# The exponential's bias taken from the maximum's own instruction, and the reciprocals' spread moved from POOL's queue to SP's

## The chip, the cores and the metric

The kernel runs on one core of one Trainium2 chip. Its time is the device time of one execution in microseconds (us); of the kernel before there are three runs, with a median of 543.97 us (543.92 to 544.14), and one execution that was also traced.

The engines are called PE (matrix multiplications), DVE (vector engine), ACT (scalar engine, here the exponential and the copies out of PSUM), POOL (a second, slower elementwise engine that also issues DMAs) and SP (which here only issues DMAs). Each runs its own list of instructions strictly in order, and waits at an instruction until the semaphores that it names have arrived.

## The reference

Three layers in a row, on 2 sequences of 768 tokens: attention with 8 heads of 64, then two mixing layers of width 512.

```
q_bits = q @ proj > 0 ; k_bits = k @ proj > 0       # 6 bits each
scores = where(q_bits == k_bits, q @ k.T / 8, -1e9) # per head, 768 x 768
attn   = exp(scores - max(scores)) ; attn /= sum(attn) + 1e-9
x      = attn @ v                                   # heads put side by side
x      = sigmoid(xr @ w_r) * (relu(xk @ w_k)**2 @ w_v)     # xk, xr mix x with the token before
h      = relu(x @ w_in) ; u, v = halves(h)
out    = (u * (w_spatial @ norm(v) + b)) @ w_out
```

The mask needs no step of its own in the kernel: signs of the projected bits stand as 12 more rows beside the 64 rows of keys and queries, scaled so that a pair of rows whose bits differ comes out of the matrix multiplication lower by 2**31 for each bit.

## The kernel before, in words

`attention` treats two heads at a time (a pair; there are 8 pairs). The work is cut into 96 units: 128 queries of one head against all 768 keys. For unit i, four functions follow each other on different engines:

- `scores(i)`: four matrix multiplications on PE into a PSUM tile `s` (two such tiles exist; lines 374 to 385).
- `peak(i)`, line 392: one DVE instruction copies `s` into an SBUF tile `p` and gives the row maximum `m` with it. `bias(i)`, line 400: a second DVE instruction, on one number per row, makes `nb`, which is `m` times -1/8.
- `expo(i)`, line 410: one ACT instruction turns `p` into exp(p/8 + nb) in place, and adds up each row into `den`.
- `transp` and `evac`, lines 420 and 426: PE transposes `p` in two halves of three blocks, and ACT copies each half from PSUM into `PT`. `av3`, line 455, then multiplies by the values, 12 matrix multiplications for half a group of 6 units.

After an opening that is written out (the string `head`), a loop runs over p = 3 to 31, three units per step. Its order is the same in each step: scores of two units, then peaks, exponentials and transposes one unit behind, `av3`, the third unit. A table `plan` adds jobs to a step: for the weights of the later layers (`weight_jobs`, lines 36 to 81: a load by SP, then ACT line 41, DVE lines 44, 49, 55, 62 and 65, ACT line 71 and two subtractions on POOL, lines 76 and 77), and for the next pair (loads by POOL, lines 239, 251 and 252, sign bits, and eight subtractions `split_piece` on POOL, line 263).

For every second step the sums of a group are inverted: `recip` (lines 435, 436, 438 on DVE, then four small DMAs by SP to DRAM, line 441), one step later `spread` (line 448: two DMAs that read that DRAM back, broadcast over 64 partitions each, into `rb`), and again a step later `finish` (line 467 on DVE: output times `rb`). Where p % 4 is 1 SP issues the spread, and where p % 4 is 3 POOL does, ahead of the jobs of the step. POOL's issue waits until the four small DMAs have landed.

`mixers` holds the two later layers; none of its code is touched.

Of the kernel before, what the change touches and what calls it, by code (L numbers as in the profile page):

```python
# [10 lines left out]
F32 = mybir.dt.float32  # L11
F32R = mybir.dt.float32r
AF = mybir.ActivationFunctionType
ALU = mybir.AluOpType
AX = mybir.AxisListType

B, H, S, D = 2, 8, 768, 64
NP = H // 2
HS = S // 2
# [3 lines left out]
BIG = float(2 ** 30)  # L23
# [59 lines left out]
def hash_attention_moe_kernel(  # L83
# [134 lines left out]
    with tc.manual_schedule():  # L218
        attention(**env)
        mixers(**env)  # L220


def attention(tc, nc, mid, dram, ident, msc, omu, misc, cst_sb, pb, epsT, kq, vP, XT, TK0, wr, w_r, wk,
              w_k, w_v, ps_s, ps_t, obank, mix_jobs, r_group, tick, now, at_tick, plan_weight, wv, **_):
    PS = bass.MemoryType.PSUM
    with ExitStack() as ctx:
        at = ctx.enter_context(tc.tile_pool(name="at", bufs=1))
# [142 lines left out]
        P, PT, den, S_ps, C_sb, R = {}, {}, {}, {}, {}, {}  # L370

        def scores(i):
            g, u = divmod(i, 6)
            pp, half = divmod(g, 2)
            e, j = divmod(u, 3)
            t = TK[pp % 2][e]
            q0 = half * HS + 128 * j
            s = ps_s.tile([128, 2, 512], F32, tag="s", name="s")
            for n in range(2):
                w = t[:, 3 - n, q0:q0 + 128]  # L380
                for c in range(2):
                    nc.tensor.matmul(  # L382
                        s[:, c, :HS], w, t[:, n, c * HS:(c + 1) * HS],
                        start=(n == 0), stop=(n == 1),
                    )
            S_ps[i] = s

        def peak(i):
            s = S_ps.pop(i)
            c = at.tile([128, 2, HS], F32, tag="p", bufs=3, name="p")  # L390
            m = at.tile([128, 1], F32, tag="m", bufs=4, name="m")
            nc.vector.tensor_scalar(  # L392
                c, s[:, :, :HS], -BIG / 2, None, op0=ALU.max, op1=ALU.max, accum_out=m
            )
            C_sb[i] = (c, m)

        def bias(i):
            c, m = C_sb[i]
            nb = at.tile([128, 1], F32, tag="nb", bufs=4, name="nb")
            nc.vector.tensor_scalar(nb, m, -0.125, None, op0=ALU.mult)  # L400
            C_sb[i] = (c, nb)

        def expo(i):
            g, u = divmod(i, 6)
            c, nb = C_sb.pop(i)
            if u == 0:
                den[g] = at.tile([128, 6], F32, tag="den", bufs=2, name="den")
                PT[g] = mid.tile([128, 2, 6, HS], F32, tag="PT", bufs=2, name="PT")
            c = c.rearrange("p c n -> p (c n)")
            nc.scalar.activation(  # L410
                c, c, AF.Exp, bias=nb, scale=0.125, accum_out=den[g][:, u:u + 1]
            )
            P[i] = c

# [18 lines left out]
        def recip(g):  # L433
            rc = rcs[g % 2]
            nc.vector.tensor_scalar_add(rc[:, 0:6], den.pop(g), 1e-9)
            nc.vector.reciprocal(rc[:, 0:6], rc[:, 0:6])
            rt = at.tile([128, 32], F32, tag="rt", bufs=2, name="rt")
            nc.vector.transpose(rt, rc)  # L438
            ds = dram.tile([6, 128], F32, tag="ds", name="ds")
            for n in range(4):  # L440
                nc.sync.dma_start(ds[:, 32 * n:32 * n + 32], rt[32 * n:32 * n + 6, :])
            R[g] = ds

        def spread(g, eng):
            ds = R[g]
            R[g] = at.tile([128, 3, 128], F32, tag="rb", bufs=2, name="rb")
            for e in range(2):
                eng.dma_start(
                    R[g][64 * e:64 * e + 64],
                    ds[3 * e:3 * e + 3].unsqueeze(0).to_broadcast([64, 3, 128]),  # L450
                )
# [11 lines left out]
        def finish(g):  # L463
            pp, half = divmod(g, 2)
            b, p = divmod(pp, NP)
            PT.pop(g)
            nc.vector.tensor_mul(
                XT[:, p, b, 1 + half * HS:1 + (half + 1) * HS],
                obank[:, :HS],
                R.pop(g).rearrange("p n q -> p (n q)"),  # L470
            )
# [15 lines left out]
        def plan_wv():  # L487
            for h in range(2):
                wv.append(mid.tile([128, 2, 4, DM], F32R, tag="PT", bufs=2, name="wv"))
                for c in range(4):  # L490
                    n = 4 * h + c
                    if not n:
                        at_tick(1, early[4])
                        at_tick(2, early[7])
                        continue
                    plan_weight(
                        (0, 0, 2, 8, 16, 18, 20, 22)[n], (wv[h][:, 0, c, :], wv[h][:, 1, c, :]),
                        w_v[128 * n:128 * n + 128],
                    )
# [13 lines left out]
        for n in range(12):  # L513
            dst, src, c, o = units[n]
# [49 lines left out]
        def av3(p):  # L564
            for n in range(3):
                av(p // 2, 3 * (p % 2) + n)

        def move(i, c, copy=nc.scalar.copy):
            evac(i, c, transp(i, c), copy)

        def score(i):
            peak(i)
            bias(i)

        ts = {}

        def group(k):
# [2 lines left out]
        def from_group(k, copy=nc.scalar.copy):  # L580
            evac(k // 2, k % 2, ts.pop(k), copy)

        def slot(n):
            for job in plan.pop((n // 10, n % 10), ()):
                job()

        step = {
            "S": scores, "K": score, "X": expo, "T": group, "E": from_group,
            "V": lambda k: from_group(k, nc.vector.tensor_copy), "J": slot, "Z": bits_mm, "G": bits_signs,
            "L": lambda e: split_part(0, e, 0, nc.vector), "R": recip, "P": lambda e: bits_place(1, (e,)),  # L590
        }
# [9 lines left out]
        for p in range(3, np3):  # L601
            a = 3 * p
            scores(a)
            scores(a + 1)
            score(a)
            if p > 3:
                move(a - 2, 1)
                expo(a)
                move(a - 1, 0)
                move(a - 1, 1)  # L610
            else:
                move(a - 1, 0)
                expo(a)
                move(a - 1, 1)
            score(a + 1)
            for job in plan.pop((p, 2), ()):
                job()
            expo(a + 1)
            av3(p - 3)
            if p % 2 == 0:  # L620
                recip(p // 2 - 1)
            if p % 4 == 3:
                spread((p - 3) // 2, nc.gpsimd)
            for job in plan.pop((p, 0), ()):
                job()
            if p % 4 == 1:
                spread((p - 3) // 2, nc.sync)
            if p >= np3 - 2:
                tick()
            scores(a + 2)  # L630
            move(a, 0)
            move(a, 1)
            score(a + 2)
            expo(a + 2)
            if p >= 4 and p % 2 == 0:
                finish((p - 4) // 2)
            move(a + 1, 0)
            for job in plan.pop((p, 1), ()):
                job()
            if p == np3 - 2:  # L640
                plan_wv()
            if p >= np3 - 2:
                tick()
# [323 lines left out]
```

## Time and profile before

| | kernel before |
|---|---|
| median of 3 runs | 543.97 us |
| the traced execution | 544.15 us |
| span of its instructions | 542.4 us |
| PE busy | 535.8 us, 99% |
| DVE busy | 379.1 us, 70% |
| ACT busy | 339.9 us, 63% |
| POOL busy | 151.9 us, 28% |
| granted clock of PE | full speed in all 40 slices of the span |

Busy shares are averages over the span. DVE and ACT are at 80 to 100% in the first 40% of it, which is the attention, and far lower behind it. A matrix multiplication is recorded with a modelled end, so rows of PE overlap a little; the start of one row against the start of the next says more than a row's length. "Idle before" in brackets names what ended an engine's wait, by the semaphore that came last.

### The profile page before, as it was taken

How to read it: one execution, taken by the hardware profiler on the slowest of the kernel's cores; microseconds unless marked ns; L12 is line 12 of the kernel's file. 1: busy time of each engine (PE TensorE's matmuls, PEld its weight loads, DVE VectorE, ACT ScalarE, POOL GpSimd, SP SyncE). 2: the span in 40 equal slices, each digit the busy share in tenths (PEclk: the TensorE clock that was granted, in tenths of full speed). 3: DMA queues.
4: the chain of work that ended last, by engine and by line, in shares of the span. 5: the costliest groups of instructions: out<-in, count | busy, mean ns of one | idle time of the engine just before them, and what ended most of it. 6: DMA issues, size and time to landing. Idle time of an engine off the chain costs nothing.

```text
span 542.4 us, 8997 instructions
## 1 busy us (share of the span) xinstructions
PE 535.8 (99%) x3174; PEld 462.4 (85%) x3174; DVE 379.1 (70%) x815; ACT 339.9 (63%) x722; POOL 151.9 (28%) x171
## 2 busy tenths in 40 slices
PE   8999999999999999999999999999999999999997
PEld 6777676767676767699999999999998999899896
DVE  8888979898979899477787776127996784443240
ACT  8988888888888889588645839147345342321211
POOL 7939585959595923100000000000200000000000
PEclk9999999999999999999999999999999999999999
DMA  8694939493949402111131111001662100001102
GB/s 245 125 231 95 242 82 228 94 246 79 233 92 250 107 24 93 55 40 39 40 116 36 44 39 40 0 1 40 211 216 78 44 25 1 2 19 40 58 21 97
DMA packets 19596, 51.10 MB, mean 94 GB/s; under 512 B 3776, under 2 KB 5984, under 8 KB 19552
## 3 DMA queue, kind: packets, MB, share of 16 engines
q0 software_dynamic: 6816, 20.45, 18.0%
q1 hardware_dynamic: 12304, 29.80, 17.6%
q8 instruction: 25, 0.41, 0.3%
q10 hardware_dynamic: 432, 0.28, 0.2%
q14 instruction: 19, 0.16, 0.1%
HBM read 46.29 MB, written 3.19 MB: 91 GB/s over the span
## 4 chain that ended last, share of the span: by engine, by line
PE 91%; DVE 5%; POOL 1%; issue 1%; ACT 1%; DVEq 0%; ACTq 0%
PE o L176 12%; PE o L455 11%; PE s L382 11%; PE k L176 11%; PE t L420 10%; PE v L721 9%; PE s L176 7%; PE w L176 6%; PE r L176 5%; PE u L176 5%; PE o L721 3%; DVE p L392 2%; PE z L280 1%; POOL tk L323 1%; ACT p L410 1%
## 5 line engine op out<-in xcount | busy, mean ns | idle before, releaser
L392 DVE TENSOR_SCALAR_CACHE_REDUCE p<-s 128x768 f32<-128x768 f32 x96 | 91.7, 955 | 19.5 <-PE s L382 17.0
L410 ACT ACTIVATE p<-p,nb 128x768 f32<-128x768 f32 x96 | 90.6, 943 | 9.6 <-DVE nb L400 8.4
L426 ACT COPY PT<-t 128x384 f32<-128x384 f32 x189 | 82.7, 476 | 16.0 <-PE t L420 15.0
L382 PE MATMUL s<-tk 128*128 128x384 f32 x384 | 85.9, 355 | 1.1 <-DVE p L392 0.7
L382 PEld LDWEIGHTS s<-tk 128*128 128x128 f32 x384 | 63.5, 188 | 21.3 <-DVE rt L438 6.0
L420 PE MATMUL t<-ident,p 128*128 128x128 f32 x576 | 76.5, 275 | 1.0 <-ACT p L410 0.7
L420 PEld LDWEIGHTS t<-ident,p 128*128 128x128 f32 x576 | 66.1, 141 | 7.8 <-ACT p L410 4.0
L455 PE MATMUL o<-PT,v 128*64 128x384 f32 x384 | 68.8, 494 | 0.0
L176 PE MATMUL k<-tk,wk 128*128 128x384 f32 x336 | 59.6, 334 | 0.0
L263 POOL TENSOR_TENSOR tk<-x,tk 64x384 fp32r<-64x384 f32 x56 | 58.4, 1073 | 1.0
L176 PEld LDWEIGHTS k<-tk,wk 128*128 128x128 f32 x336 | 58.4, 188 | 0.0
L721 PE MATMUL v<-k,wv 128*128 128x384 f32 x288 | 53.6, 334 | 0.0
L721 PEld LDWEIGHTS v<-k,wv 128*128 128x128 f32 x288 | 50.3, 188 | 0.0
L780 POOL DMA_DIRECT2D wsp<-in_w_spT_dram x6 | 3.6, 618 | 165.8 <-DVE w_a L44 159.3
L455 PEld LDWEIGHTS o<-PT,v 128*64 128x64 f32 x384 | 24.8, 136 | 28.6 <-issue 28.2
L176 PE MATMUL o<-wk,tk 128*128 128x512 f32 (+1 forms) x168 | 36.2, 374 | 0.0
L176 PEld LDWEIGHTS o<-wk,tk 128*128 128x128 f32 x168 | 30.0, 188 | 5.5
L702 ACT ACTIVATE kr<-k 128x384 f32<-128x384 f32 x28 | 13.6, 487 | 29.6 <-PE k L176 29.4
L121 ACT CAST tk<-g 128x384 fp32r<-128x384 f32 x16 | 8.2, 514 | 37.5 <-DVE g L851 37.5
L176 PE MATMUL w<-wk,tk 128*128 128x512 f32 x132 | 30.7, 390 | 0.0
L176 PE MATMUL r<-tk,wr 128*128 128x384 f32 x168 | 30.6, 337 | 0.0
L687 DVE TENSOR_TENSOR k<-kt,k 128x384 fp32r<-128x384 f32 x32 | 17.8, 555 | 17.9 <-ACT k L705 17.6
(117 smaller groups left out, 878.9 us busy)
## 6 DMA issues: line engine op xcount, KB each, us to landing
tk<-in_kq_dram POOLq DMA_DIRECT2D x30, 384.0 KB, 9.0
x<-in_kq_dram POOLq DMA_DIRECT2D x6, 768.0 KB, 7.8
w_raw<-in_w_k_dram SPq DMA_DIRECT2D x8, 512.0 KB
w_raw<-in_w_v_dram SPq DMA_DIRECT2D x8, 512.0 KB
w_raw<-in_w_in_dram SPq DMA_DIRECT2D x8, 512.0 KB
v<-in_vP_dram SPq DMA_DIRECT2D x8, 384.0 KB
out_dram<-ot SPq DMA_DIRECT2D x11, 256.0 KB
wsp<-in_w_spT_dram POOLq DMA_DIRECT2D x6, 384.0 KB, 5.1
```

The source lines that it names most:

```text
L121: nc.scalar.copy(hi, src)
L176: nc.tensor.matmul(o, a, x, start=(i == 0), stop=(i == len(seq) - 1))
L263: nc.gpsimd.tensor_sub(tk[l, 1 + 2 * t, o], raw[pp][l, t, o], tk[l, 2 * t, o])
L382: nc.tensor.matmul(s[:, c, :HS], w, t[:, n, c * HS:(c + 1) * HS], start=(n == 0), stop=(n == 1),)
L392: nc.vector.tensor_scalar(c, s[:, :, :HS], -BIG / 2, None, op0=ALU.max, op1=ALU.max, accum_out=m)
L410: nc.scalar.activation(c, c, AF.Exp, bias=nb, scale=0.125, accum_out=den[g][:, u:u + 1])
L420: nc.tensor.transpose(t[:, 128 * n:128 * n + 128], p[:, k0:k0 + 128], ident)
L426: copy(PT[g][:, e, 3 * c:3 * c + 3, 128 * j:128 * j + 128], t[:, :HS].rearrange("p (n q) -> p n q", n=3),)
L455: nc.tensor.matmul(obank[64 * e:64 * e + 64, :HS], vt[g // 2][:, kt, e, :], PT[g][:, e, kt, :], start=(kt == 0), stop=(kt == 5),)
L687: later(lag, lambda: eng.tensor_sub(lo, src, hi))
L702: nc.scalar.activation(r, o[:, :HS], AF.Relu)
L721: nc.tensor.matmul(os[m][:, :HS], w, x, start=(c == 0 and k == 0), stop=(c == 7 and k == 2),)
```

## The change

The first DVE instruction now multiplies the scores by -1/8 and takes the minimum with 2**26 (a bound that only the masked scores reach), and its running result over the row is the minimum: this is already minus the maximum over 8, the bias. `bias` and its tile `nb` are gone, and the exponential runs with scale -1 and bias `m`. Of the spreads that POOL issued, only the one of step 3 stays there; those of steps 7, 11, 15, 19, 23, 27 and 31 are issued by SP, behind the step's jobs.

```diff
             nc.vector.tensor_scalar(
-                c, s[:, :, :HS], -BIG / 2, None, op0=ALU.max, op1=ALU.max, accum_out=m
+                c, s[:, :, :HS], -0.125, BIG / 16, op0=ALU.mult, op1=ALU.min, accum_out=m
             )
-        def bias(i):
-            c, m = C_sb[i]
-            nb = at.tile([128, 1], F32, tag="nb", bufs=4, name="nb")
-            nc.vector.tensor_scalar(nb, m, -0.125, None, op0=ALU.mult)
-            C_sb[i] = (c, nb)
...
             nc.scalar.activation(
-                c, c, AF.Exp, bias=nb, scale=0.125, accum_out=den[g][:, u:u + 1]
+                c, c, AF.Exp, bias=m, scale=-1.0, accum_out=den[g][:, u:u + 1]
             )
...
-            score(a)
+            peak(a)
...
-            if p % 4 == 3:
+            if p == 3:
                 spread((p - 3) // 2, nc.gpsimd)
             for job in plan.pop((p, 0), ()):
                 job()
-            if p % 4 == 1:
+            if p % 2 and p > 3:
                 spread((p - 3) // 2, nc.sync)
```

On DVE, this is the list before from step 7 to the first peak of step 9 (line 392 is the peak, 400 the bias, 62, 65, 44, 49 and 55 the weights, 435 to 438 the inversion):

```order
L62 TENSOR_SCALAR w_p<-w_b 128x512
L392 TENSOR_SCALAR p,m<-s 128x768
L400 TENSOR_SCALAR nb<-m 128x1
L65 SCALAR_TENSOR_TENSOR w_a<-w_raw,w_p 128x512
L392 TENSOR_SCALAR p,m<-s 128x768
L400 TENSOR_SCALAR nb<-m 128x1
L392 TENSOR_SCALAR p,m<-s 128x768
L400 TENSOR_SCALAR nb<-m 128x1
L435 TENSOR_SCALAR rc_90<-den 128x6
L436 RECIPROCAL rc_90<-rc_90 128x6
L438 STREAM_TRANSPOSE rt<-rc_90 128x32
L44 TENSOR_SCALAR w_a<-w_a 128x512
```

And the same place now, where the lines from 400 on have moved up (435 is now 429, 467 now 461):

```order
L62 TENSOR_SCALAR w_p<-w_b 128x512
L392 TENSOR_SCALAR p,m<-s 128x768
L65 SCALAR_TENSOR_TENSOR w_a<-w_raw,w_p 128x512
L392 TENSOR_SCALAR p,m<-s 128x768 x2
L429 TENSOR_SCALAR rc_90<-den 128x6
L430 RECIPROCAL rc_90<-rc_90 128x6
L432 STREAM_TRANSPOSE rt<-rc_90 128x32
L44 TENSOR_SCALAR w_a<-w_a 128x512
```

The biases are gone and nothing else has changed its place on DVE. On POOL, at step 7, the two spread DMAs between the subtractions for the next pair (263) and the load of the pair after it (239) are gone, and the weights' subtractions (76, 77) stand nearer to line 263:

```order
 L263 TENSOR_TENSOR tk_0_77<-x,tk_0_77 64x384 x4
 L263 TENSOR_TENSOR tk_1_78<-x,tk_1_78 64x384 x4
-L448 DMA rb<-ds 64x384 x2
 L239 DMA x<-in_kq_dram 128x2x768
 L76 TENSOR_TENSOR w_b<-w_b,wr 128x512
```

On SP, at the same step, they come in ahead of a weight's load (37) and the values' load (257):

```order
-L441 DMA ds<-rt 6x32 x4
+L435 DMA ds<-rt 6x32 x4
+L442 DMA rb<-ds 64x384 x2
 L37 DMA w_raw<-in_w_r_dram 128x1024
 L257 DMA v<-in_vP_dram 128x768
```

There the two DMAs stand directly behind the four whose data they read (435, 441 before).

## Rows read from the trace of the kernel before

**Rows 1.** The page's chain of waits: shares of the span by engine.

```profile
PE 91%; DVE 5%; POOL 1%; issue 1%; ACT 1%; DVEq 0%; ACTq 0%
```

**Rows 2.** Groups by line: xcount | busy us, mean ns | idle before.

```profile
L392 DVE TENSOR_SCALAR_CACHE_REDUCE p<-s 128x768 f32<-128x768 f32 x96 | 91.7, 955 | 19.5 <-PE s L382 17.0 <-ACT wr L71 1.5
...
L400 DVE TENSOR_SCALAR nb<-m 128x1 f32<-128x1 f32 x96 | 14.8, 154 | 3.3
...
L44 DVE TENSOR_SCALAR w_a<-w_a 128x512 f32<-128x512 f32 x32 | 14.1, 440 | 4.9 <-ACT w_a L41 4.9
```

**Rows 3.** Timeline of PE, line 455: start us, us, engine line operation.

```profile
77.28 2.16 PE L455 MATMUL o<-PT,v 128*64 128x384 f32 x12
...
83.64 2.16 PE L455 MATMUL o<-PT,v 128*64 128x384 f32 x12
...
90.81 2.16 PE L455 MATMUL o<-PT,v 128*64 128x384 f32 x12
...
190.89 2.16 PE L455 MATMUL o<-PT,v 128*64 128x384 f32 x12
...
198.55 2.16 PE L455 MATMUL o<-PT,v 128*64 128x384 f32 x12
...
205.37 2.16 PE L455 MATMUL o<-PT,v 128*64 128x384 f32 x12
```

**Rows 4.** Timeline of one unit's peak, bias and exponential, DVE and ACT.

```profile
62.16 0.95 DVE L392 TENSOR_SCALAR_CACHE_REDUCE p<-s 128x768 f32<-128x768 f32 x1
...
63.03 0.08 DVE L392 DVE_READ_ACCUMULATOR p<-s 128x1 f32 x1
63.15 0.15 DVE L400 TENSOR_SCALAR nb<-m 128x1 f32<-128x1 f32 x1
63.25 0.96 DVE L392 TENSOR_SCALAR_CACHE_REDUCE p<-s 128x768 f32<-128x768 f32 x1
63.52 0.94 ACT L410 ACTIVATE p<-p,nb 128x768 f32<-128x768 f32 x1
```

**Rows 5.** Timeline of DVE and PE from 80 to 89 us, steps 11 and 12.

```profile
80.47 0.96 DVE L392 TENSOR_SCALAR_CACHE_REDUCE p<-s 128x768 f32<-128x768 f32 x1 [1.48 <-ACT wr L71]
...
81.54 0.68 DVE L65 SCALAR_TENSOR_TENSOR w_a<-w_raw,w_p 128x512 f32<-128x512 uint32 x1
...
84.33 0.56 DVE L435 TENSOR_SCALAR rc<-den 128x6 f32<-128x6 f32 x1
...
85.29 1.21 DVE L44 TENSOR_SCALAR w_a<-w_a 128x512 f32<-128x512 f32 x1
...
88.65 0.97 PE L382 MATMUL s<-tk 128*128 128x384 f32 x4 [0.27 <-DVE p L392]
...
88.71 0.56 DVE L467 TENSOR_TENSOR XT<-o,rb 128x384 f32<-128x384 f32 x1
```

**Rows 6.** Timeline of POOL in the same stretch.

```profile
81.64 1.16 POOL L448 DMA_DIRECT2D rb<-ds  x2 [1.79 <-DMA ds<-rt]
...
82.77 0.77 POOL L239 DMA_DIRECT2D x<-in_kq_dram  x1
...
83.54 1.32 POOL L76 TENSOR_TENSOR w_b<-w_b,wr 128x512 f32<-128x512 f32 x1
...
84.93 1.28 POOL L77 TENSOR_TENSOR wr<-w_b,w_a 128x512 fp32r<-128x512 f32 x1
```

**Rows 7.** Timeline of DVE and of POOL at steps 27 and 28.

```profile
188.78 2.22 DVE L65 SCALAR_TENSOR_TENSOR w_a<-w_raw,w_p 128x512 f32<-128x512 uint32 x1
...
193.09 0.16 DVE L435 TENSOR_SCALAR rc<-den 128x6 f32<-128x6 f32 x1
...
189.12 1.32 POOL L76 TENSOR_TENSOR w_b<-w_b,wk 128x512 f32<-128x512 f32 x1
```

**Rows 8.** The chain of waits in the opening: start us, us, what.

```profile
17.51 0.17 DVE nb L400
```

**Rows 9.** Timeline of SP's queue, the spread of step 9.

```profile
67.90 1.27 SPq L448 DMA_DIRECT2D rb<-ds  x2
```

More of the change, by code (lines that the diff above doesn't have):

```diff
@@ L392, in peak @@
             nc.vector.tensor_scalar(
-                c, s[:, :, :HS], -BIG / 2, None, op0=ALU.max, op1=ALU.max, accum_out=m
+                c, s[:, :, :HS], -0.125, BIG / 16, op0=ALU.mult, op1=ALU.min, accum_out=m
             )
             C_sb[i] = (c, m)
-        def bias(i):
-            c, m = C_sb[i]
-            nb = at.tile([128, 1], F32, tag="nb", bufs=4, name="nb")
-            nc.vector.tensor_scalar(nb, m, -0.125, None, op0=ALU.mult)
-            C_sb[i] = (c, nb)
         def expo(i):
             g, u = divmod(i, 6)
-            c, nb = C_sb.pop(i)
+            c, m = C_sb.pop(i)
             if u == 0:
@@ L569, in move @@
             evac(i, c, transp(i, c), copy)
-        def score(i):
-            peak(i)
-            bias(i)
         ts = {}
@@ L587, in attention @@
         step = {
-            "S": scores, "K": score, "X": expo, "T": group, "E": from_group,
+            "S": scores, "K": peak, "X": expo, "T": group, "E": from_group,
             "V": lambda k: from_group(k, nc.vector.tensor_copy), "J": slot, "Z": bits_mm, "G": bits_signs,
@@ L614, in attention @@
                 move(a - 1, 1)
-            score(a + 1)
+            peak(a + 1)
             for job in plan.pop((p, 2), ()):
@@ L632, in attention @@
             move(a, 1)
-            score(a + 2)
+            peak(a + 2)
             expo(a + 2)
```

## The prediction

> **What bounds the kernel now.** I read the chain of waits first. It runs through PE for 91% of the span and through DVE for 5% [rows 1]. Behind about 232 us it holds nothing but PE, so the later layers follow the end of the attention one for one, and only the attention and its opening can gain.
>
> Then I read PE's timeline by the starts of the value products (line 455), which come once per step. A regular step takes 83.64 - 77.28 = 6.36 us [rows 3]; a step with the sign bits of the next pair (every fourth) takes 0.78 more, and I count it as regular. The reader is to look for steps that are longer:
>
> - 83.64 to 90.81 is 7.17, a stall of 0.81; the same place eight steps later has 7.10, a stall of 0.74.
> - The places between them in the pattern (steps 9, 17 and 25) have 6.76, 6.75 and 6.69: stalls of 0.40, 0.39 and 0.33.
> - 190.89 to 198.55 is 7.66, a stall of 1.30, and 198.55 to 205.37 is 6.82, a stall of 0.46.
>
> Together 4.43 us. That is nearly all that PE loses between 24 and 212 us, and so the ceiling of the gain there.
>
> Third, who is late at these places. Before the stall at 88.65 PE waits for a peak on DVE [rows 5]. DVE was in step at 80.47, where it had itself been waiting for 1.48 us, and has no gap after that. So within these 8 us DVE has too much to do, while over a regular step it has time left: a stall is what DVE falls behind in one such stretch. Two of its rows there are far longer than their work: line 435, 0.56 here against 0.16 when POOL is idle [rows 5, 7], and line 44, 1.21 against a mean of 0.44 [rows 2, 5]. Both end just as POOL's line 76 or 77 ends (83.54 + 1.32 = 84.86; 84.93 + 1.28 = 86.21) [rows 6]. At the four other places of this kind line 435 takes 0.86, 0.85, 1.21 and 0.81, again up to the end of POOL's line 77.
>
> **The bias.** 96 instructions of 154 ns leave DVE [rows 2]. What one costs is less, since rows overlap. The peak at 62.16 and the next at 63.25 are 1.09 apart, and the accumulator's readout between them ends at 63.11 [rows 4]. The next peak could start between 63.03 and 63.18, so a bias costs 0.07 to 0.19; I take 0.11, the nearest to the peaks' own 0.95 plus a short gap. The exponential starts 0.22 behind the bias' end (63.30 to 63.52), and would start 0.22 behind the readout: 0.19 earlier for each unit.
>
> The peak itself gets a multiplication and a minimum in place of two maxima. No row shows that pair in this form. Its nearest rows are the peak as it is, 955 ns for 768 numbers, and line 44, which has two operations with two constants and no row longer than its work but those that meet POOL [rows 2]. I take no change.
>
> **POOL's queue.** Seven spreads leave it. At step 11 POOL had ended line 263 at 81.64 - 1.79 = 79.85, and then waited for the small DMAs and spent 1.16 on the issue [rows 6]. Now line 239 follows at 79.85, line 76 at 80.62, and it ends near 81.94. This makes a new meeting: DVE's line 65, due at 81.43, reads and writes SBUF at the same time as line 76. The trace has one case of it: at 188.78 line 65 takes 2.22 instead of 0.68, and ends 0.56 behind the end of line 76 [rows 5, 7]. So line 65 would end at 81.94 + 0.56 = 82.50 instead of 82.22, a loss of 0.28. Line 77 needs line 65's result, starts near 82.6 and ends by 83.9, before line 435 (about 84.3) and before line 44: both run free.
>
> The Trainium skill speaks against the change here (SBUF — State Buffer, section "Who interferes with whom"): a DVE instruction with two inputs in SBUF contends with a GpSimd instruction that reads SBUF, and whoever issues first keeps the shared ports for its whole instruction. By that rule line 65 loses what is left of line 76, and nothing where it starts first. The row at 188.78 disagrees with the last part: line 65 began 0.34 ahead of line 76 and still ended behind it, so I price by the row.
>
> Sum for DVE up to the late peak of step 12: four biases -0.44, line 435 -0.40, line 44 -0.77, line 65 +0.28, in all -1.33 against a stall of 0.81. By the same steps the other places have:
>
> - near 61, 114 and 167 us: -0.44, line 435 -0.65 to -0.70, line 65 +0.35 to +0.40: about -0.7 against 0.40, 0.39 and 0.33;
> - near 141 us: -0.44, -1.05, +0.40: -1.1 against 0.74;
> - near 195 us: line 76 starts 1.2 earlier, so that line 65 ends near 189.8 instead of 191.00: -1.2, and three biases -0.33: -1.5 against 1.30;
> - at 205 us: three biases -0.33, and DVE no longer comes from a stall of 1.30: 0.46 goes.
>
> Every stall is covered, by 0.2 to 0.5. These covers are no larger than the doubt on line 65, so I count nine tenths of 4.43: 4.0 us. Exponentials that start 0.19 earlier add to the cover, and PE is the next to be late, which is the bound.
>
> **The opening.** Between 16.5 and 21.5 us the chain goes through peaks, biases (the row at 17.51) and exponentials [rows 8]. Three biases in a row, two at 0.11 on DVE and one at 0.19 in front of ACT, are 0.4, of which ACT's own list may hide some: 0.3, with 0 and 0.5 as ends.
>
> **SP's queue.** The spread costs SP 1.27 where it has it already [rows 9]. At step 11 it would be issued at 81.64 and end at 82.91; the reader, line 467, comes at 88.71 [rows 5, 6], nearly 6 us later. Behind it stand a weight's and the values' load, about 0.6 us later than now; their readers are one to two steps of 6.36 away. Nothing waits; without that cover, `finish` would hold DVE for what is missing.
>
> **Sum.** 544.15 (the traced execution: a span of 542.4 and 1.75 around it) - 4.0 - 0.3 = 539.85. The traced execution lies 0.18 above the median of the runs, so 539.7 us is what I expect of the runs.
>
> **Rivals.**
>
> - Half the gain. POOL's subtractions come to lie elsewhere than I think, and hold line 65 and then again line 435. Then each place keeps only its biases: 0.44, or 0.33 near 195 and 205. That still clears 0.40, 0.39 and 0.33 and takes 0.44 + 0.44 + 0.33 + 0.33 off the others: 2.66, with the opening 3.0, and 541.0. For it: the covers are small. Against it: line 77 has 0.4 us to spare before line 435.
> - Slower. Line 76 starts just inside line 65 at the five places where it used to come later, as at 188.78, and line 65 pays the full 2.22 - 0.68 = 1.54; line 77 follows it and still holds line 435. Net +1.54 - 0.44 = 1.1 at each, 5.5 in all, less 0.3 in the opening and 0.4 near 195: 548.8. It decides from the point where line 65 loses more than the biases and the freed locks give, about 1.1. Against it: line 76 starts 0.8 ahead of line 65, so at most 0.5 is left of it.
> - No change. PE's stalls end with ACT: an exponential is the last thing waited for behind some of them, and ACT, not DVE, would be late by the same. Against it: ACT had idle time before those very exponentials, waiting for a bias. 543.9.
>
> **Chances.** The forecast 0.78, half the gain 0.14, no change 0.04, slower 0.04. A difference of about 0.2% (1.1 us) can be told from none. The first two are both faster; some of the second's lower tail is not, so faster 0.92, same 0.04, slower 0.04. The range: the low end is all 4.43, the 0.5 of the opening and a little of the tail of the attention, 538.9; the high end takes in the half gain with one place failing, 541.6.
>
> **What would show it.** Line 400 is absent, the peak stays at 0.95 to 0.96, and peaks back to back come 0.97 to 1.0 apart. Line 435 (429 after) takes near 0.16 at steps 8, 12, 16, 20 and 24, and POOL's line 77 has ended before it. Line 65 is longer by 0.3 to 0.5 at steps 7 to 23, and no longer 2.22 at step 27. The value products come every 6.36 us, or 7.14 with sign bits, without exception. A peak longer than 0.96, a line 65 of 2 us at several steps, or SP's spread landing behind line 467 would make the forecast wrong.

## The result and the profile after

| | before | after |
|---|---|---|
| median (4 runs each) | 543.94 us | 539.20 us |
| range of the runs | 543.68 to 544.14 | 539.04 to 539.66 |
| ratio, 95% interval | | 0.9914 (0.9897 to 0.9932) |
| the traced execution | 544.15 us | 539.66 us |
| its span | 542.4 us | 537.9 us |

The changed kernel is 4.7 us faster. Its page answers to [rows 1] and [rows 2] like this (busy time by engine; the chain's shares; a group by line, mean in ns behind the comma):

```profile
PE 533.0 (99%) x3174; PEld 463.4 (86%) x3174; DVE 358.0 (67%) x719; ACT 339.0 (63%) x722; POOL 144.2 (27%) x157
...
PE 98%; ACT 0%; DVE 0%; issue 0%; POOL 0%; POOLq 0%
...
L392 DVE TENSOR_SCALAR_CACHE_REDUCE p<-s 128x768 f32<-128x768 f32 x96 | 90.8, 954 | 36.0 <-PE s L382 33.7
```

The chain runs through PE for 98% where it was 91%, and DVE's 5% are gone. A peak takes 954 ns against 955, so a multiplication with a minimum costs what two maxima did. DVE now waits 33.7 us for scores (17.0 before): it is early where it was late.

PE's value products, the answer to [rows 3] (start us, us, engine, line and operation):

```profile
76.89 2.16 PE L449 MATMUL o<-PT,v 128*64 128x384 f32 x12
...
83.24 2.16 PE L449 MATMUL o<-PT,v 128*64 128x384 f32 x12
...
89.59 2.16 PE L449 MATMUL o<-PT,v 128*64 128x384 f32 x12
...
188.16 2.16 PE L449 MATMUL o<-PT,v 128*64 128x384 f32 x12
...
194.51 2.16 PE L449 MATMUL o<-PT,v 128*64 128x384 f32 x12
...
200.88 2.16 PE L449 MATMUL o<-PT,v 128*64 128x384 f32 x12
```

The steps that took 7.17, 7.66 and 6.82 take 6.35, 6.35 and 6.37. I call "stall" what a step takes beyond its regular 6.36 (7.14 with sign bits). All the stalls of the loop together were 4.64 us and are 0.09. The first value product comes at 24.38 instead of 24.45. From the end of the loop to the last layers nothing has changed: from 211.85 to 231.57 were 19.72 us, from 207.23 to 226.96 are 19.73. So of 4.49 us between the two traced executions, 4.55 come from the stalls and 0.07 from the opening, and 0.13 were lost again outside both, nearly all of it in the later layers (310.79 us from there to the end before, 310.90 after).

How a stall went is best seen at steps 7 to 9, the first place. Before, DVE, POOL, PE and ACT (columns as above; idle time before a row in brackets):

```profile
51.35 1.10 DVE L62 TENSOR_SCALAR w_p<-w_b 128x512 uint32<-128x512 uint32 x1
...
54.91 0.68 DVE L65 SCALAR_TENSOR_TENSOR w_a<-w_raw,w_p 128x512 f32<-128x512 uint32 x1
...
55.85 1.32 POOL L76 TENSOR_TENSOR w_b<-w_b,wr 128x512 f32<-128x512 f32 x1
...
57.02 2.16 PE L455 MATMUL o<-PT,v 128*64 128x384 f32 x12
...
57.25 1.28 POOL L77 TENSOR_TENSOR wr<-w_b,w_a 128x512 fp32r<-128x512 f32 x1
...
57.70 0.86 DVE L435 TENSOR_SCALAR rc<-den 128x6 f32<-128x6 f32 x1
...
60.61 0.95 DVE L392 TENSOR_SCALAR_CACHE_REDUCE p<-s 128x768 f32<-128x768 f32 x1
...
61.85 0.94 ACT L410 ACTIVATE p<-p,nb 128x768 f32<-128x768 f32 x1 [0.55 <-DVE nb L400]
```

And after, with SP's queue:

```profile
51.07 0.42 DVE L62 TENSOR_SCALAR w_p<-w_b 128x512 uint32<-128x512 uint32 x1
...
53.47 1.16 SPq L442 DMA_DIRECT2D rb<-ds  x2
...
54.42 1.31 POOL L76 TENSOR_TENSOR w_b<-w_b,wr 128x512 f32<-128x512 f32 x1
...
54.71 1.57 DVE L65 SCALAR_TENSOR_TENSOR w_a<-w_raw,w_p 128x512 f32<-128x512 uint32 x1
...
56.43 1.28 POOL L77 TENSOR_TENSOR wr<-w_b,w_a 128x512 fp32r<-128x512 f32 x1 [0.70 <-DVE w_a L65]
...
57.00 2.16 PE L449 MATMUL o<-PT,v 128*64 128x384 f32 x12
...
57.97 0.28 DVE L429 TENSOR_SCALAR rc<-den 128x6 f32<-128x6 f32 x1
...
60.36 0.95 DVE L392 TENSOR_SCALAR_CACHE_REDUCE p<-s 128x768 f32<-128x768 f32 x1
...
61.42 0.94 ACT L404 ACTIVATE p<-p,m 128x768 f32<-128x768 f32 x1
```

Line 77 ends at 57.71 instead of 58.53, and line 435 (now 429) no longer waits for it. Line 65 has become longer by 0.89. The peak starts 0.25 earlier, and the exponential 0.43 earlier, since its start now follows the peak's by 1.06 instead of 1.24. That just covers this place's stall of 0.40.

### The profile page after: what moved, and what is told of

Read it like the earlier page. It is cut to its first block, busy times and chain, and to the rows that moved or that the text cites. A ratio compares the mean times of both kernels' runs of the same rounds, so it can differ in the third digit from the quotient of the medians.

```text
span 537.9 us, 8836 instructions
## 1 busy us (share of the span) xinstructions
PE 533.0 (99%) x3174; PEld 463.4 (86%) x3174; DVE 358.0 (67%) x719; ACT 339.0 (63%) x722; POOL 144.2 (27%) x157
## 4 chain that ended last, share of the span: by engine, by line
PE 98%; ACT 0%; DVE 0%; issue 0%; POOL 0%; POOLq 0%
PE s L382 13%; PE o L176 12%; PE o L449 12%; PE t L414 12%; PE k L176 11%; PE v L711 9%; PE s L176 7%; PE w L176 6%; PE r L176 6%; PE u L176 5%; PE o L711 3%; PE z L280 1%; PE o L272 1%; ACT tk L321 0%; DVE zb L287 0%; ACT p L404 0%
## 5 line engine op out<-in xcount | busy, mean ns | idle before, releaser
L392 DVE TENSOR_SCALAR_CACHE_REDUCE p<-s 128x768 f32<-128x768 f32 x96 | 90.8, 954 | 36.0 <-PE s L382 33.7
L404 ACT ACTIVATE p<-p,m 128x768 f32<-128x768 f32 x96 | 90.6, 944 | 1.6 <-DVE p L392 0.5
L382 PE MATMUL s<-tk 128*128 128x384 f32 x384 | 84.7, 354 | 0.1
L414 PE MATMUL t<-ident,p 128*128 128x128 f32 x576 | 74.5, 273 | 0.2 <-ACT p L404 0.2
L176 PEld LDWEIGHTS r<-tk,wr 128*128 128x128 f32 x168 | 29.0, 188 | 1.4 <-ACT PT L420 0.6
```

What stands on the lines that cost most here:

```text
L176: nc.tensor.matmul(o, a, x, start=(i == 0), stop=(i == len(seq) - 1))
L382: nc.tensor.matmul(s[:, c, :HS], w, t[:, n, c * HS:(c + 1) * HS], start=(n == 0), stop=(n == 1),)
L392: nc.vector.tensor_scalar(c, s[:, :, :HS], -0.125, BIG / 16, op0=ALU.mult, op1=ALU.min, accum_out=m)
L404: nc.scalar.activation(c, c, AF.Exp, bias=m, scale=-1.0, accum_out=den[g][:, u:u + 1])
L414: nc.tensor.transpose(t[:, 128 * n:128 * n + 128], p[:, k0:k0 + 128], ident)
```

## The experiments

Medians of several runs; the kernel before ran in the same sessions, with 543.63 us (542.78 to 545.18) beside e1 to e4 and 543.31 (542.30 to 545.25) beside a2, e5, e6 and e7. Ratios are to it. Kernels that ran once more ran a single time and have no ratio. Stalls are those of the one traced execution.

**Each part alone.** The first kernel (e1) is the changed one with the old rule of the spreads:

```diff
-            if p == 3:
+            if p % 4 == 3:
                 spread((p - 3) // 2, nc.gpsimd)
...
-            if p % 2 and p > 3:
+            if p % 4 == 1:
                 spread((p - 3) // 2, nc.sync)
```

> The kernel after, but POOL issues the spread at p % 4 == 3 again, as before. Theory (both edits are needed: the bias gives DVE time, the moved spread frees line 429 and line 44 from POOL's lines 76 and 77): the three stalls of 0.3 to 0.4 us shrink to 0.1 or less, near 88 us about 0.4 to 0.5 stays, near 141 us 0.3 to 0.4, near 196 us 0.8 to 1.0 with line 65 at 2 us and more again; 540.8 to 541.6 in all. Rival 1 (the bias alone does it, POOL's place is of no account): no stall, 539.2. Rival 2 (the spread alone does it): 543.9, all stalls as before.

The second (e2) is the kernel before with the new rule:

```diff
-            if p % 4 == 3:
+            if p == 3:
                 spread((p - 3) // 2, nc.gpsimd)
...
-            if p % 4 == 1:
+            if p % 2 and p > 3:
                 spread((p - 3) // 2, nc.sync)
```

> The kernel before (two DVE instructions per unit, with the bias) with the moved spreads alone. Theory: line 435 is down to 0.16 to 0.3 us at steps 8, 12, 16, 20 and 24 and line 65 up to about 1.6 at the steps before them, so the small stalls near 62, 116 and 170 us stay at 0.3 to 0.5, those of 0.8 and 0.7 fall to 0.2 to 0.4, that of 1.3 to 0.3 or less, the one behind it stays near 0.3; 541.5 to 542.5. Rival 1 (the bias alone does it): 543.9. Rival 2 (the spread alone does it): 539.5. Rival 3 (line 65 against line 76 costs more than the freed locks give): slower than before, 544.5 or more.

| | us | ratio, 95% interval | stalls in the traced execution |
|---|---|---|---|
| e1, bias alone | 540.80 | 0.9946 (0.9932 to 0.9960) | 1.84 |
| e1 once more, one run | 540.62 | | 1.59 |
| e2, spreads alone | 540.61 | 0.9944 (0.9931 to 0.9957) | 1.28 |
| the change again (a2) | 539.09 | 0.9919 (0.9903 to 0.9935) | 0.04 |

Either part alone gives about 3 us, and both give 4.2, not 6: each stall needs a little, and either part brings most of it. e1 came out at the low end of what I had expected, e2 below it (541.5 to 542.5): its line 65 takes 1.24 to 1.33 at steps 7 to 23, not 1.6. In e1 POOL still holds the inversion at three of the five places in either trace, at step 16 longer than before (start us, us; DVE before, then POOL and DVE of e1):

```profile
111.39 0.85 DVE L435 TENSOR_SCALAR rc<-den 128x6 f32<-128x6 f32 x1
```

```profile
109.52 1.27 POOL L77 TENSOR_TENSOR wk<-w_b,w_a 128x512 fp32r<-128x512 f32 x1
...
109.56 1.27 DVE L429 TENSOR_SCALAR rc<-den 128x6 f32<-128x6 f32 x1
```

Line 429 ends at 110.83, behind the end of line 77 at 110.79. Counted from the value product of the step, DVE came to it 0.26 earlier (0.42 behind it, 0.68 before), by the biases that are gone, and then stood there for longer. So the biases ahead of line 435 give nothing where this hold stands.

In e2 the hold is gone: line 435 takes 0.16, and the exponential starts 4.61 behind the value product of step 8 (before: 61.85 - 57.02 = 4.83), though it still waits for a bias. DVE, PE and ACT:

```profile
54.63 1.33 DVE L65 SCALAR_TENSOR_TENSOR w_a<-w_raw,w_p 128x512 f32<-128x512 uint32 x1
...
56.73 2.16 PE L455 MATMUL o<-PT,v 128*64 128x384 f32 x12
...
58.05 0.16 DVE L435 TENSOR_SCALAR rc<-den 128x6 f32<-128x6 f32 x1
...
60.10 0.95 DVE L392 TENSOR_SCALAR_CACHE_REDUCE p<-s 128x768 f32<-128x768 f32 x1
...
61.34 0.94 ACT L410 ACTIVATE p<-p,nb 128x768 f32<-128x768 f32 x1 [0.33 <-DVE nb L400]
```

One stall of e1 was of another kind: 1.25 between the value products of steps 25 and 26, where PE waited 1.17 for a load of x that had taken 11.18 us. To see whether it belongs to the kernel, e1 ran a second time. 

> The bias-only kernel once more. Theory (PE's wait of 1.17 us for the next pair's x at step 25 of its first profile was one late transfer, 11.2 us from issue to landing): it is not there again, or at another step, and the stalls that DVE makes add up to 0.4 to 0.8 again. Rival (POOL's late issue of that load at step 23 makes it each time): 1.0 us or more at step 25 again.

It did not come again (stalls of 0.16, 0.21, 0.32, 0.24 and 0.47 at steps 13 to 29), so it was one late transfer in that execution; the second trace is the one that shows e1's order: 1.6 us of stalls left.

**The bias' time, or its delay.** The changed kernel with the bias instruction put back on DVE and its result unread (e3).

```diff
             C_sb[i] = (c, m)
+            nb = at.tile([128, 1], F32, tag="nb", bufs=4, name="nb")
+            nc.vector.tensor_scalar(nb, m, -0.125, None, op0=ALU.mult)
```

> The kernel after with the old bias instruction put back behind each peak, its result read by nobody: DVE's time for it is back, the exponential still starts from the peak. Theory (DVE's time is what was short, the exponential's earlier start only adds to the cover): most of the loss of the spread-only kernel returns, 541 to 542, with stalls at the same steps. Rival (the 0.19 us of the exponential's earlier start is what counts): no stall, 539.2 to 539.5.

539.87 us, 0.9929 (0.9915 to 0.9943), stalls 0.42: between the two, and nearer to the rival; my theory was wrong. DVE, PE and ACT at the place of the rows above:

```profile
56.80 2.16 PE L451 MATMUL o<-PT,v 128*64 128x384 f32 x12
...
60.19 0.95 DVE L392 TENSOR_SCALAR_CACHE_REDUCE p<-s 128x768 f32<-128x768 f32 x1
...
61.25 0.94 ACT L406 ACTIVATE p<-p,m 128x768 f32<-128x768 f32 x1 [0.15 <-DVE p L392]
```

Against e2, which has as many instructions of the same length on DVE, the difference is that the exponential doesn't wait for the bias: it starts 1.06 behind the peak's start instead of 1.24, and 1.28 of stalls become 0.42, so 0.86 us are the exponential's earlier start. Against the changed kernel (0.09), the biases' own time on DVE is worth 0.33, nearly all of it at steps 30 and 31 (0.18 and 0.12); at steps 9 to 29 no stall of e3 is above 0.02. These sizes are those of single executions: by the medians e2 and e3 are 0.74 apart, and e3 and the changed kernel, which ran beside other runs, 0.67 to 0.78, so the medians don't show which of the two is the larger.

The traces give a plain rule for the places at steps 9, 13, 17, 21 and 25. Take the start of the first exponential of the step, counted from the value product of the step before: 4.77 to 5.24 in the kernel before, 4.50 to 4.61 in e2, 4.35 to 4.46 in e3, 4.41 to 4.43 in the changed kernel. What it lies beyond 4.43 is the stall, within 0.02, in all four and in e1. So the changed kernel is just on time: e2's 4.50 already stalls by 0.07. The peak ahead of that exponential starts equally early in e2 (3.26 to 3.36 behind the value product) and in the changed kernel (3.36 to 3.38), biases or not.

**All spreads on SP.** That of step 3 too.

```diff
-            if p == 3:
-                spread((p - 3) // 2, nc.gpsimd)
...
-            if p % 2 and p > 3:
+            if p % 2:
```

> The kernel after, with the spread of step 3 on SP too, so that POOL issues none. Theory: no stall stands near step 4 in the kernel after, PE runs through there, so nothing is to be had: 539.2, within 0.2. Rival (SP's queue is full in the opening with the 8 placing DMAs of the second pair, and the spread or the loads behind it come late): a wait of line 461 or of a first product in steps 4 to 6, 539.5 to 541.

539.66 us, 0.9926 (0.9913 to 0.9940); stalls 0.76, of which 0.30 at step 6 and 0.50 at step 9. This is the rival's time, and all of its runs (539.50 to 540.12) lie above those of a2 (538.93 to 539.26), which ran beside other runs. Ahead of step 6 line 41 on ACT waits 0.72 for a weight's load, which SP issued behind the spread at 28.74 (27.86 in the changed kernel). The stall at step 9 comes from line 65 at step 7 (DVE and POOL):

```profile
54.41 2.11 DVE L65 SCALAR_TENSOR_TENSOR w_a<-w_raw,w_p 128x512 f32<-128x512 uint32 x1
...
54.64 1.32 POOL L76 TENSOR_TENSOR w_b<-w_b,wr 128x512 f32<-128x512 f32 x1
```

Here line 65 starts 0.23 ahead of line 76 and pays nearly the 1.54 of the row at 188.78 [rows 7]; in the changed kernel it starts 0.29 behind line 76 and pays 0.89. The slower rival's mechanism is that near.

**The changed kernel again**, in the second group of runs (its result is in the table above). 

> The kernel after, unchanged, on the chip and beside the runs of the next three. 539.0 to 539.7; no stall in the loop of more than 0.1 us. What differs from its first profile, the start of the opening above all, is what one execution differs from another.

**Is it the hold?** The changed kernel with line 76 and 77 of every second weight behind the four loads for the next pair, so that they come late again, with the biases gone and the spreads on SP.

```diff
-            plan_unit(4 + 2 * n, soon if n % 2 else late, ld, jobs)
+            plan_unit(4 + 2 * n, soon if n % 2 else late, ld, jobs, range(7 if n % 2 else 8))
+            if n % 2:
+                held.append((4 + 2 * n + 2, jobs[7]))
...
+        for p, job in held:
+            at_slot(p, 0, job)
```

> The kernel after, with POOL's lines 76 and 77 of steps 7, 11, 15, 19, 23 put behind the four loads of the next pair, so that they no longer meet line 65, but again lines 429, 44 and 49. Theory (what POOL holds up on DVE between step 7 and step 9 makes the stall, wherever it is): line 65 is back at 0.69, and 1.0 to 2.0 us of waiting comes back on 429, 44, 49 or 55 behind it, closer to the peak that PE waits for; stalls of 0.2 to 0.8 us at steps 9, 13, 17, 21, 25; 540.5 to 542.5. Rival (without the biases DVE has so much room that POOL's holds no longer reach PE): no stall, 539.2 to 539.7.

548.32 us, 1.0074 (1.0050 to 1.0098): slower than the kernel before by 5. In its traced execution (545.17 us, the fastest of its runs) line 429 takes 0.61 to 1.22, up to the ends of lines 76 and 77, and line 44 up to 1.22 again, 0.28 beyond line 77's, and the stalls are 5.77. That is outside the 540.5 to 542.5 expected, and not all of the stalls lie at the places of the hold, so it ran once more. 

> The kernel with POOL's subtractions behind the loads once more; its profiled execution of 545.2 us was the fastest of runs up to 548.9. Theory (the loads of x and of the pair start at the same time as the weights' subtractions and land late in some executions): the stalls of DVE and POOL as in its first profile, 5 to 6 us in all, and 2 to 3 us more in waits for a DMA. Rival: all of the 548 lies in waits on DVE and POOL.

548.19 us, stalls 9.23. Transfers in its chain of waits (start us, us from issue to landing), and ACT, DVE and PE in its timeline:

```profile
54.87 10.93 DMA w_raw<-in_w_r_dram
...
82.34 9.96 DMA rb<-ds
```

```profile
65.88 0.67 ACT L41 ACTIVATE w_a<-w_raw 128x512 f32<-128x512 f32 x1 [1.12 <-DMA w_raw<-in_w_r_dram]
...
92.40 0.56 DVE L461 TENSOR_TENSOR XT<-o,rb 128x384 f32<-128x384 f32 x1 [3.34 <-DMA rb<-ds]
...
93.01 1.19 PE L449 MATMUL o<-PT,v 128*64 128x384 f32 x6 [1.87 <-DVE XT L461]
```

Counted from the value product of their step, the pair's loads now start 2.7 to 3.4 us earlier, beside x and a weight. The spread by SP took 9.96 us to land, its reader waited 3.34, and PE 1.87. So this kernel shows two effects, the hold and late transfers. Its first trace keeps them apart: 3.81 of the 5.77 lie at steps 9, 13, 17, 21 and 25, where the peak starts 3.73 to 4.36 behind the value product (3.36 to 3.38 in the changed kernel), behind lines 429 and 44 that are held again, and the rule of the exponential's start gives these stalls within 0.08. The other 1.88, at steps 10, 14 and 22, stand behind three loads of weights that took 10.71 to 11.34 us. The time of the kernel as a whole doesn't measure the hold. The kernel does show that the six microseconds that SP's spread has to spare in the changed kernel hang on what else is being loaded.

**Can line 65 or the biases alone move the stall?** The kernel before, with line 65 of every second weight one place earlier in the table.

```diff
-        soon = ((-1, 2), (-1, 0), (-1, 0), (0, 0), (1, 0), (1, 0), (1, 1), (1, 1))
+        soon = ((-1, 2), (-1, 0), (-1, 0), (0, 0), (1, 0), (1, 0), (1, 0), (1, 1))
```

> The kernel before with one job moved: line 65 of every second weight stands directly behind line 62, in front of the peak where DVE waits 1.4 us for PE anyway; biases and POOL's spreads as before. Theory (the stalls are what DVE falls behind within steps 7 to 9, 11 to 13 and so on, and any 0.7 us taken out of such a stretch does the same as the change): stalls of 0.40, 0.39, 0.33 gone, those of 0.81 and 0.74 down to 0.3 or less, that of 1.30 to 0.3 or less, 0.46 smaller; 540.0 to 541.2. Rival (the biases or the exponential's start behind them are what PE waits for): 543.5 to 544.

542.96 us (12 runs), 0.9989 (0.9978 to 1.0000): nearly no gain, and neither the theory's time nor the rival's. In the traced execution (542.17) the stalls at steps 9, 13, 17, 21 and 25 are still 0.32, 0.46, 0.46, 0.72 and 0.38; the 1.30 at step 29 is gone, since line 65 no longer meets line 76 there, and that at step 13 is smaller, where line 76 comes earlier and line 435 takes 0.21. 0.7 us of DVE's work behind the first peak went away, and this is why it gives nothing (DVE and POOL):

```profile
52.35 1.38 DVE L65 SCALAR_TENSOR_TENSOR w_a<-w_raw,w_p 128x512 f32<-128x512 uint32 x1
...
55.42 0.96 DVE L392 TENSOR_SCALAR_CACHE_REDUCE p<-s 128x768 f32<-128x768 f32 x1 [0.53 <-PE s L382]
...
57.08 1.28 POOL L77 TENSOR_TENSOR wr<-w_b,w_a 128x512 fp32r<-128x512 f32 x1
...
57.60 0.79 DVE L435 TENSOR_SCALAR rc<-den 128x6 f32<-128x6 f32 x1
```

The second peak, which in the kernel before followed line 65 without a wait, now waits 0.53 for PE's scores. So DVE comes to line 435 no earlier than before, 0.68 to 0.69 behind the value product, at this place and at the four others alike, and is held there again: line 435 ends at 58.39, line 77 at 58.36. What DVE saved was lost in a wait for PE ahead of the hold. The run doesn't show what the hold would have done with it; e1 does.

**The opening.** The changed kernel with one tile of the sign bits in a buffer that is free at that time, so that DVE needn't wait for it.

```diff
-            b1 = at.tile([128, HS], F32, tag="zb", name="zb")
+            b1 = mid.tile([128, 512], F32, tag="w_a", bufs=2, name="zb")[:, :HS]
```

> The kernel after, with the sign bits of the first pair's second head in another buffer (that of a weight, not yet used), so that the second pair's signs on DVE need not wait 0.82 us for POOL's placing at 16 us. Theory (in the opening the chain runs through DVE at that place): 0.2 to 0.5 us less, 538.8 to 539.3, the first value product 0.2 to 0.5 nearer to the first scores. Rival (ACT's list of exponentials and copies is as long in that stretch): no change.

538.96 us, 0.9917 (0.9902 to 0.9932): 0.13 below a2, which the runs can't tell from none. Line 287 comes 0.8 earlier (15.19, against 16.01 in the changed kernel), and the next peak now waits 0.79 for PE and starts at 16.59 (16.55 in the changed kernel; DVE):

```profile
15.19 0.61 DVE L287 TENSOR_SCALAR zb<-z,msc 128x384 f32<-128x384 f32 x1
...
16.59 0.96 DVE L392 TENSOR_SCALAR_CACHE_REDUCE p<-s 128x768 f32<-128x768 f32 x1 [0.79 <-PE t L414]
```

From the third unit's scores to the first value product its trace has 14.39 us, against 14.59 and 14.55 in the two of the changed kernel: 0.2 or a little less, at the low end of the theory, in one execution.

**The kernel before again**, for its stalls from one execution to another. 

> The kernel before once more, to see what one execution differs from another. Theory (its stalls are the DVE and POOL meetings at fixed steps, the spread of its runs, 542.3 to 545.3, comes from transfers that land at other times): the eight stalls at the same steps within 0.1 to 0.3 us, and the opening or a wait for a DMA different. Rival: stalls at other steps, other in size.

543.75 us, with the same eight stalls (0.12 at step 31, 0.32 to 1.21 at the other seven, 4.54 in all).

## Why the prediction was right, step by step

It was right in the time (539.7 against 539.2), in the places of the gain, and in that both edits bring it. Within it, some terms were mis-sized, and one reason was wrong. That every stall went although the terms were off was in part luck: the changed kernel is on time by less than 0.1 us at five places, where the prediction counted on covers of 0.3 to 0.5.

- **The ceiling** of 4.43 us in seven stalls: right. With one of 0.12 at step 31 and smaller ones it is 4.64; of it 4.55 went. To count only nine tenths was too few.
- **Who is late.** The prediction said that DVE has too much to do in those 8 us, and counted four biases of 0.11 ahead of the late peak. This step failed. DVE is late at steps 9 to 25 because line 435 ends with POOL's line 76 or 77, or line 44 0.29 behind line 77 (86.50 and 86.21; the prediction read it as ending with it), and at step 29 because line 65 ends 0.56 behind line 76. Work taken out ahead of such a hold comes to nothing while it stands (e1: 1.27 instead of 0.85 at step 16), and with the holds on 435 and 44 gone the time of all the biases on DVE leaves no stall above 0.02 at these places (e3). The sum credits a bias twice as well: line 65 was to end at 82.50 behind POOL, whatever came ahead of it, and the bias ahead of it was still counted. The chance of half the gain was reckoned by the same step: "each place keeps only its biases". e1 came out there (540.8 against 541.0), but for another reason: what its places kept is the exponential's earlier start (1.05 behind the peak's instead of 1.24), and at two of five places in either trace line 429 starts outside POOL's row or near its end (0.17 to 0.37).
- **The bias.** 0.11 each on DVE lies inside what was seen, but 0.97 to 1.0 from one peak to the next does not describe it. Of 25 pairs of peaks back to back, 11 are 0.84 to 0.88 apart (56.21 and 57.09, for one), 13 are 1.02 to 1.05 and one is 0.97, from mostly 1.09 or 1.10 with a bias; so a bias costs 0.04 to 0.26. The prediction's own rows give 0.07 to 0.22 (63.25 less 63.18 and 63.03), not 0.19. All 96 together are worth 0.33 us of stalls in e3's trace. The exponential's earlier start of 0.19, which I gave no price and called cover, is worth 0.86 by the traces of e2 and e3.
- **POOL's queue.** At step 11 the forecast was line 76 at 80.62, line 65's end at 82.50, line 77 from 82.6 to 83.9, all ahead of line 435. The rows after: POOL and DVE, with the answer to [rows 5, 6].

```profile
80.67 1.31 POOL L76 TENSOR_TENSOR w_b<-w_b,wr 128x512 f32<-128x512 f32 x1
80.94 1.60 DVE L65 SCALAR_TENSOR_TENSOR w_a<-w_raw,w_p 128x512 f32<-128x512 uint32 x1
82.69 1.28 POOL L77 TENSOR_TENSOR wr<-w_b,w_a 128x512 fp32r<-128x512 f32 x1 [0.70 <-DVE w_a L65]
...
84.22 0.28 DVE L429 TENSOR_SCALAR rc<-den 128x6 f32<-128x6 f32 x1
...
84.90 0.48 DVE L44 TENSOR_SCALAR w_a<-w_a 128x512 f32<-128x512 f32 x1
...
87.49 0.55 DVE L461 TENSOR_TENSOR XT<-o,rb 128x384 f32<-128x384 f32 x1
```

  Line 65 ends at 82.54, 0.56 behind line 76, as the row at 188.78 had it [rows 7]. But it starts at 80.94, since DVE is 0.49 earlier than I had let it be, and so it loses 0.92 and not 0.28. The end was right and the loss mis-sized, for the reason of the point above: an end that POOL sets takes up what DVE has gained ahead of it. The Trainium skill (SBUF — State Buffer, section "Who interferes with whom") has it that the later of the two waits out the earlier (GpSimd there is POOL here). Line 76 is first here, by 0.27; a wait for its whole length would let line 65 end at 81.98 + 0.68 = 82.66, and it ends at 82.54, so this row agrees to 0.12. The rows at 188.78 and, in e4, at 54.41 do not: there line 65 is first and still ends 0.56 behind line 76.
- **What comes free.** Lines 435 and 44 nearly as predicted (0.56 to 0.28 where I had said near 0.16, 1.21 to 0.48). The prediction left two more out. Line 435 took 0.81 to 0.95 at the inversions between these (steps 6 to 26, every fourth) and takes 0.16 to 0.17 there. And line 62, held by POOL's line 263 at steps 7 to 27 (1.10 above), comes 0.28 earlier at step 7 and takes 0.42 to 0.44. Both stay long in e2 (0.82 to 0.90, and 0.87 to 1.06), so it is the biases' absence that frees them: DVE comes there just ahead of POOL's next row, not inside it. In e3 the same instruction is held at those inversions as before (0.87 to 0.97), and no stall follows there. The groups by line after (count | busy us, mean ns | idle before):

```profile
L65 DVE SCALAR_TENSOR_TENSOR w_a<-w_raw,w_p 128x512 f32<-128x512 uint32 x32 | 27.1, 846 | 0.9
...
L62 DVE TENSOR_SCALAR w_p<-w_b 128x512 uint32<-128x512 uint32 x32 | 13.6, 424 | 0.3
L429 DVE TENSOR_SCALAR rc<-den 128x6 f32<-128x6 f32 x16 | 4.0, 251 | 0.0
```

  Before they were 23.6, 16.9 and 10.6 us: line 65 costs 3.5 more, the two others 9.9 less.
- **The covers** of 0.2 to 0.5 were too large, since line 65's loss was taken too small: at step 9 the exponential came 0.43 earlier against 0.40 of stall. The sum held because errors of opposite signs met: the biases credited ahead of the late peak and line 65's loss on the one side, the exponential's start without a price on the other. That is luck, not foresight.
- **The opening,** 0.3: right. From the third unit's scores to the first value product it is 14.86 and 14.93 in two executions of before, 14.59 and 14.55 in two of after, and 14.86 in e2, which keeps the bias. In the pair of traced executions only 0.07 is to be seen, since the scores themselves began 0.20 later.
- **SP's spread:** right here. At the place that the prediction priced it is issued at 80.27, and line 461 comes to it at 87.49 without a wait. e5 shows the condition.
- **The rivals.** The slower one needed line 65 to pay 1.54 at five places and line 77 to hold line 435; it pays 0.9 and line 77 is done in time. "No change, because ACT would be late" is excluded by the result, though it had something in it: what PE waits for in the end is the start of the exponential.

What stays open: the runs of the kernel before spread more (542.3 to 545.3) than those of the changed one (538.9 to 539.7). Two traced executions of before have the same stalls to 0.1, so I can't say which of them changes from run to run.

## What to carry to other kernels

When an engine is late, look at which of its instructions is longer than its work and at whose end it ends: work removed ahead of such an instruction is lost in it, and only what lies behind it, or what moves the other engine's end, counts, unless so much goes that the instruction starts ahead of the other engine's. Two edits that clear the same small stalls do not add up; run each alone before either is credited with the sum. And a small instruction between two engines (here a bias of 0.15 us) has two prices, the time that it takes and the start that it delays (here 0.33 and 0.86 us by the traces): work out both. Between two traces count times from a row of the same step, since an execution as a whole can begin some tenths of a us earlier.

## What the runs showed of the hardware

- Where line 62 is held it ends 0.28 to 0.29 behind the piece of POOL's line 263 in which it starts (in the kernel before at 52.45, the piece from 51.16 to 52.17). A start shortly ahead of such an end shows no hold: at 51.07 in the changed kernel, with a piece that ends at 51.19, it takes its plain 0.42, although the next piece begins at 51.15.
- A DVE instruction with two inputs can be held by one on POOL that starts after it: line 65 took 2.22, 2.11 and 2.17 us instead of 0.68 where line 76 began 0.34, 0.23 and 0.27 later (the kernel before at 188.78, e4 at 54.41, e1 once more at 186.31), and each time it ended 0.56 behind line 76.
- The same transfer can take very different times: loads of x land in 5 to 11 us, and a spread of 96 KB, for which the changed kernel leaves 6 us without a wait, took 9.96 where it was issued beside a pair's loads (e5). That this company is the cause is not shown by itself.
